# Linear attention into a Swish layer on one core: one order for all pieces, denominators from a gram product, loads by token quarter

## The chip, the cores and the metric

The kernel runs on 1 core of one Trainium2 chip. The metric is device time in microseconds (us), the median of the runs. TensorE (PE) multiplies matrices; VectorE (DVE), ScalarE (ACT) and GpSimd (POOL) do the elementwise work; SyncE (SP) issues most of the loads and stores. Each engine works through its own instructions strictly in the order in which the program gives them, and waits on semaphores for the others.

## The reference

Inputs are q, k, v of shape (4 batches, 4 heads, 1088 tokens, 32), two 8x32 matrices S1 and S2, and the layer's w_in (128x2048), w_out (2048x128) and beta (2048).

```python
def phi(x):                                  # 64 features of a token
    a = einsum('rd,bhsd->bhsr', S1, x)
    b = einsum('rd,bhsd->bhsr', S2, x)
    return einsum('bhsi,bhsj->bhsij', a, b).reshape(..., 64)
q_p, k_p = phi(q), phi(k)
kv = einsum('bhsf,bhsd->bhfd', k_p, v)
z = sum(k_p, axis=2)
x = einsum('bhsf,bhfd->bhsd', q_p, kv) / (einsum('bhsf,bhf->bhs', q_p, z) + 1e-6)
x = x.transpose(0, 2, 1, 3).reshape(4352, 128)
h = x @ w_in
out = (h / (1 + exp(-beta * h))) @ w_out
```

The sum over tokens in kv and z runs over a whole batch and head, so no token of a batch has its x before all of that batch's k and v are in.

## The kernel before

**The layer.** beta is folded into the weights: winp = w_in times beta, woutp = w_out divided by beta, both f16, so that g = silu(x winp) and out = g woutp. The 4352 tokens make nine chunks, eight of 512 and one of 256. Each chunk has eight waves, 72 in all. A wave is W (`w1`, L388: two 512-wide matmuls, in the first four waves four 256-wide ones, into one of two PSUM buffers `wave`), G (`silu`, L404: ACT reads that buffer and writes g in f16, six buffers) and V (`w2`, L419: the matmuls into `moeout`). O (`turn_out`, L433) turns a finished chunk on DVE and SP stores it. I call the nth of each W0, W1 and so on, from 0. W8 is the first wave of the second chunk and needs tokens 512 to 1023 in xT.

**The attention.** DVE turns k and q in blocks of 32x32 (`turn_k`, L442; `turn_q`, L448), PE projects them with S1 and S2 (`kps`, `qps`, L478), DVE turns the projections token by token (`turn_ab`, L499), and `outer` (L507, on POOL or DVE) multiplies a by b into the 64 features. `kv` (L555) multiplies features of k with v over the tokens. In batches 2 and 3 z is the sum of k's features on POOL (`sum_z`, L741 to L745), and the features of q are turned back (`turn_qo`, L518) for two matmul groups, `den_g` (L832) and `num_g` (L846); DVE inverts the denominators (`invert`, `spread_rc`, L767 to L782) and multiplies (`divide_g`, L857). In batch 1 and the second part of batch 0, called chunks B, C and D, the features of q never become token-major: `spread` (L531) makes a and b feature by feature in PSUM, ACT or DVE copies one (`asb`, L542), DVE multiplies (`mult`, L548), and `den0` (L756) and `num0` (L791) follow; batch 1's z comes from a gram product of its k projections on PE (`gram`, L692; `gram_z`, L714). The first 512 tokens of batch 0 (two halves of 256) take squares instead: products a*b as differences of two squares (`spread_sq`, L665; `square`, L674; `sq_mm`, L680); their z comes from k^T k on PE (`kk`, L576, 136 instructions) through `kk_s2`, `z_terms`, `z_sum` (L595 to L614).

**The order of the work** is written out by hand: `ORDER` (L1117) is a list of names, and every name emits its instructions, DMAs included, at that place. A leading point marks the pieces of the start. It begins with warm matmuls on unused data (`keep_warm`, L204: six ahead of the list, two in it).

**Loads.** At the top of the program SP issues nearly all of them at once: batch 0's k in two parts with beta and half of q between, v of batch 0 by head (four DMAs of 144 KB, `load_v`, L143), half of w_in and w_out, the rest of q, and so on through batch 2. A wait of one load on SP holds all that stand behind it.

Of the kernel before, what the change touches and what calls it, by code (L numbers as in the profile page):

```python
# [9 lines left out]
F32 = mybir.dt.float32  # L10
F16 = mybir.dt.float16
ACTF = mybir.ActivationFunctionType
MUL = mybir.AluOpType.mult

P = 128
# [3 lines left out]
def kernel(  # L19
# [12 lines left out]
    nc = tc.nc  # L32
# [10 lines left out]

    NJK = 9
    TH = T // 2
# [4 lines left out]

    NA = 16
    q_chk = {"B": (0, 16, 9), "C": (1, 0, 9), "D": (1, 18, 8)}
    QW = 32 * 9
    NJ0 = 5
    HA = 16 * NA

    QB = [0, 9, 16, 25]
    JW = 32 * NJK
    JR = [(0, 2), (2, 4), (4, 6), (6, 9)]
    WARM0 = 6  # L60
# [4 lines left out]
    ld = ctx.enter_context(tc.tile_pool(name="ld", bufs=3))  # L65
# [9 lines left out]

# [20 lines left out]
    beta4 = sb([P, DFF // 4], F32, "beta4")  # L96
# [3 lines left out]
    s12 = sb([2 * R, H, D], F32, "s12")  # L100
# [3 lines left out]
    def load_s(n, s_, eng):  # L104
        eng.dma_start(
            out=s12[R * n : R * n + R],
            in_=bass.AP(tensor=s_.tensor, offset=s_.offset, ap=[[D, R], [0, H], [1, D]]),
        )

    load_s(0, S1, nc.scalar)  # L110
    load_s(1, S2, nc.scalar)
    k_t, q_t, v_t = {}, {}, {}

    def load_rows(src, dst, b, tag, parts=((0, T),)):
        if b not in dst:
            dst[b] = ld.tile([P, TPAD, D], F32, tag=tag, name=tag)
        for t0, t1 in parts:
            nc.sync.dma_start(
                out=dst[b][:, t0:t1, :],
                in_=bass.AP(  # L120
                    tensor=src.tensor,
                    offset=src[b, 0].offset + t0 * D,
                    ap=[[T * D, P], [1, (t1 - t0) * D]],
                ),
            )

    def load_k0(j0, j1):
        if 0 not in k_t:
            k_t[0] = ld.tile([P, TPAD, D], F32, tag="k", name="k")
        nc.sync.dma_start(  # L130
            out=cut(k_t[0], [[NJK * D, 4], [1, (j1 - j0) * D]], j0 * D),
            in_=bass.AP(
                tensor=k.tensor,
                offset=k[0, 0].offset + j0 * D,
                ap=[[T * D, P], [NJK * D, 4], [1, (j1 - j0) * D]],
            ),
        )

    def load_v(b):
        t = v_t[b] = ld.tile([P, H, NJK, D], F32, tag="v", name="v")  # L140
        if b < B - 1:
            for h in range(H):
                nc.sync.dma_start(  # L143
                    out=t[:, h],
                    in_=bass.AP(
                        tensor=v.tensor, offset=v[b, h].offset, ap=[[NJK * D, 4], [T * D, 32], [1, NJK * D]]
                    ),
                )
            return
        nc.gpsimd.memset(t[96:, :, NJK - 2 :, :], 0.0)  # L150
        for g in range(4):
# [10 lines left out]
    def load_win(c0, c1):  # L162
        nc.sync.dma_start(out=w_in_sb[:, c0:c1], in_=moe_w_in[:, c0:c1])

    beta_bc = sb([P, DFF // 2], F32, "beta_bc")

    def load_beta():
        nc.sync.dma_start(
            out=bass.AP(
                tensor=beta4.tensor,  # L170
                offset=beta4.offset,
                ap=[[32 * beta4.ap[0][0], 4], [1, DFF // 4]],
            ),
            in_=moe_beta.rearrange("(r c) -> r c", r=4),
        )

    def load_wout(j0, j1):
        nc.sync.dma_start(
            out=w_out_sb[:, j0:j1, :],
            in_=moe_w_out[j0 * P : j1 * P, :].rearrange("(j p) m -> p j m", p=P),  # L180
        )

    load_k0(0, NJ0)
    load_beta()
    load_rows(q, q_t, 0, "q", ((0, NA),))
    load_k0(NJ0, NJK)
    load_v(0)
    load_win(0, DFF // 2)
    load_wout(0, NJ // 2)
    load_rows(q, q_t, 0, "q", ((NA, T),))  # L190
    load_rows(k, k_t, 1, "k")
    load_win(DFF // 2, DFF)
    load_wout(NJ // 2, NJ)
    load_rows(q, q_t, 1, "q")
    load_v(1)
    load_rows(k, k_t, 2, "k")
    load_rows(q, q_t, 2, "q")
    load_v(2)


    def keep_warm(n):
        t = bank(1, "warm")
        for _ in range(n):
            nc.tensor.matmul(out=t, lhsT=idle, rhs=cut(idle, [[0, 4], [1, P]]), start=True, stop=True)  # L204
# [3 lines left out]
    nc.gpsimd.dma_start(out=beta_jp, in_=moe_beta.rearrange("(j p) -> j p", p=P))  # L208
    ones = sb([P, P], F32, "ones")
    nc.vector.memset(ones, 1.0)  # L210
    silu0 = sb([P, 1], F32, "silu0")
    nc.scalar.activation(out=silu0, in_=ones[:, :1], func=ACTF.Silu)

    hm = sb([P, 2], F32, "hm")
# [3 lines left out]
    gm = sb([P, 4], F32, "gm")  # L218
    nc.vector.memset(gm, 0.0)
    for c in range(4):  # L220
        nc.vector.memset(gm[32 * c : 32 * c + 32, c : c + 1], 1.0)
    pm = sb([P, 2], F32, "pm")
    nc.vector.memset(pm[:, 0:1], 0.25)
    nc.vector.memset(pm[:, 1:2], -0.25)
    sg = sb([P, 2], F32, "sg")
    nc.vector.memset(sg, 0.0)
    nc.vector.memset(sg[:64, 0:1], 4.0)
    nc.vector.memset(sg[64:, 1:2], -4.0)
    sgs = sb([P, 1], F32, "sgs")
    nc.vector.memset(sgs[:64], 4.0)  # L230
    nc.vector.memset(sgs[64:], -4.0)
    eps = sb([P, 4 * NJK], F32, "eps")
    nc.vector.memset(eps, 1e-6)
    e3 = sb([P, 3], F32, "e3")
    nc.vector.memset(e3, 0.0)
    nc.vector.memset(e3[:, 1:2], 1.0)
# [4 lines left out]
    zb = [sb([P, H, 32], F32, f"zb{n}") for n in range(2)]  # L241
    mk = sb([P, H, R], F32, "mk")
    zbg = [sb([P, H, 2, 32], F32, f"zbg{n}") for n in range(2)]

    def clear():
        for n in range(2):
            nc.gpsimd.memset(kT2[n][:, T:, :], 0.0)
        for n in range(2):
            nc.gpsimd.memset(zb[n], 0.0)
            nc.gpsimd.memset(zbg[n], 0.0)  # L250
        nc.gpsimd.tensor_tensor(
            out=mk,
            in0=cut(ident, [[2 * R, H], [1, R]]),
            in1=cut(ident, [[2 * R, H], [1, R]], 64),
            op=mybir.AluOpType.add,
        )

    keep_warm(WARM0)
# [5 lines left out]
    spm = sb([P, 2, R, R], F32, "spm")  # L264
    s1pm = sb([P, 2 * R], F32, "s1pm")
    sab = [sb([P, R, R], F32, f"s{n}") for n in range(2)]

    def spread_s():
        t = bank(2, "srep")
        nc.tensor.matmul(  # L270
            out=t[:, : 2 * R],
            lhsT=s12.rearrange("p h d -> p (h d)"),
            rhs=ident[: 2 * R, : 2 * R],
            is_transpose=True,
            start=True,
            stop=True,
        )
        PS["srep"] = t
# [4 lines left out]
    def s_block():  # L283
        nc.gpsimd.tensor_tensor(
# [3 lines left out]
    def s_sums():  # L288
        ADD, SUB = mybir.AluOpType.add, mybir.AluOpType.subtract
        for n, op in enumerate((ADD, SUB)):  # L290
            nc.gpsimd.tensor_tensor(
                out=spm[:, n], in0=cut(st, [[1, R], [0, R]]), in1=cut(st, [[0, R], [1, R]], R), op=op
            )

    def s_pairs():
        nc.gpsimd.tensor_tensor(
# [5 lines left out]
        nc.gpsimd.tensor_tensor(  # L302
            out=s1pm.rearrange("p (m c) -> p m c", m=2),
            in0=cut(st, [[0, 2], [1, R]]),
            in1=cut(pm, [[1, 2], [0, R]]),
# [3 lines left out]
    def spread_factors():  # L309
        for n in range(2):  # L310
            nc.gpsimd.tensor_copy(out=sab[n], in_=cut(st, ([[1, R], [0, R]], [[0, R], [1, R]])[n], n * R))

    def beta_mm(n, dst):
        row = slice(32 * n, 32 * n + 1)
        nc.tensor.matmul(out=dst, lhsT=ones[row, :], rhs=beta4[row, :], start=True, stop=True)
# [5 lines left out]
    def prep_win(c0, c1, scale=None, eng=None):  # L321
        (eng or nc.gpsimd).tensor_tensor(  # L322
            out=winp[:, c0:c1],
            in0=beta_bc[:, c0:c1] if scale is None else scale,
            in1=w_in_sb[:, c0:c1],
            op=MUL,
        )

    def prep_rbeta():
        bt = bank(0, "bt")  # L330
# [3 lines left out]
        PS["bt"] = bt  # L334
# [14 lines left out]

    xT = sb([P, NTOK], F16, "xT")  # L350

# [11 lines left out]
    ALT = 6  # L363

# [17 lines left out]
    def w1():  # L382
        wave = ci, t0, o, w, j0, jn, head, tail = waves[moe["w"]]
        per = jn // 2
        wv = psm.tile([P, 2, TCH], F32, tag="wave", name="wave")
# [12 lines left out]
    def silu():  # L398
# [4 lines left out]
        gw = per * w  # L403
        nc.scalar.activation(out=g[:, :, :gw], in_=wv[:, :, :gw], func=ACTF.Silu)  # L404
        moe["todo"].append((wave, [g[:, jj // per, (jj % per) * w : (jj % per + 1) * w] for jj in range(jn)]))
        moe["g"] += 1

    def w2():
        wave, g = moe["todo"].pop(0)
        ci, t0, o, w, j0, jn, head, tail = wave  # L410
        if head:
            if ci >= ALT and (ci - ALT) % 2:
                t = pools()["ps1"].tile([P, TCH], F32, tag="one", name="moeout1")
# [26 lines left out]

    def turn_k(b, t0=0, t1=T):
# [11 lines left out]
    PS, KP, QO, QT, QP, ND, KAB, QAB, ASB, KVZ, KVD, RB = ({} for _ in range(12))  # L453

    def wave2(name):
        return psm.tile([P, 2, 512], F32, tag="wave", name=name)

    late = {}

    def pools():  # L460
        if not late:
            start.close()
            for n in ("ps2", "ps1", "pso"):
# [700 lines left out]
```

## Time and profile before

| | us |
|---|---|
| median of 3 runs | 115.93 (115.67 to 115.98) |
| span of the profiled execution | 116.5 |
| PE busy, 1316 matmul instructions | 105.3 |
| DVE busy | 57.5 |
| ACT busy, of it 72 silus | 79.9, 66.6 |
| POOL busy | 42.9 |
| HBM read and written | 8.94 MB, 2.23 MB |

The profiled execution has no time of its own beside its span, the time from its first to its last instruction; that stands 0.5 us above the median of the runs. A line of the timeline gives start, duration, engine, line, operation, tiles (out<-in) and shape, and in brackets the idle time before it and who ended it. An f32 matmul counts as two instructions. A busy PE is not PE at its peak, since its records overlap. The mean granted clock of the execution is 0.971 of full speed.

### The profile page before, as it was taken

To read this page: it belongs to the slowest core of one execution; us is meant where nothing else is said; L and a number is where in the kernel's file an instruction comes from. 1 tells how busy PE (TensorE), PEld (TensorE's weight loads), DVE (VectorE), ACT (ScalarE), POOL (GpSimd) and SP (SyncE) were. 2 spreads that over 40 slices of the span, in tenths; PEclk is the share of its full clock that TensorE was granted. 3 is DMA by queue.
4 is the path that set the end of the run, shared out by engine and by line. 5 is a ranking of instruction groups with operands and counts; after the bars stand their busy time and mean duration, and the time that the engine had idled before them with its cause. 6 is when DMAs were issued, how large, how long until landed. Compare 5 with 4: busy or idle time off the path is not lost.

```text
span 116.5 us, 3190 instructions
## 1 busy us (share of the span) xinstructions
PE 105.3 (90%) x1316; PEld 48.8 (42%) x1316; DVE 57.5 (49%) x122; ACT 79.9 (69%) x107; POOL 42.9 (37%) x61
## 2 busy tenths in 40 slices
PE   6898179898899999999999999999999989999960
PEld 2276055234434443344343354454344434444540
DVE  4384003588499754887899483529087020020210
ACT  4037002486868977555787975999986999999950
POOL 4036069230960099999399974000000000000000
PEclk9999955799999999999999999999999999999999
DMA  2859998279229975202300014005001303213242
GB/s 62 232 153 253 286 355 286 107 200 239 103 101 214 213 202 151 37 0 43 53 8 0 0 17 75 4 0 90 6 0 32 58 0 52 44 17 62 35 69 45
DMA packets 25046, 11.37 MB, mean 98 GB/s; under 512 B 18612, under 2 KB 23748, under 8 KB 25032
## 3 DMA queue, kind: packets, MB, share of 16 engines
q1 hardware_dynamic: 24376, 11.09, 38.8%
q8 instruction: 10, 0.16, 0.6%
q10 hardware_dynamic: 624, 0.07, 0.4%
q14 instruction: 4, 0.03, 0.1%
q0 software_dynamic: 32, 0.01, 0.1%
HBM read 8.94 MB, written 2.23 MB: 96 GB/s over the span
## 4 chain that ended last, share of the span: by engine, by line
PE 75%; DMA 10%; DVE 6%; SPq 4%; issue 2%; DVEq 0%
PE wave L388 25%; PE moeout L419 24%; DMA v<-in_v_dram 8%; PE kvz L555 5%; PE nps L846 3%; PE dps L832 2%; PE aps L531 2%; PE bps L531 2%; DVE o_sb L433 2%; DMA out_dram<-o_sb 2%; PE nps L791 2%; PE dps L756 2%; PE ndps L750 1%; SPq L143 1%; SPq L372 1%
## 5 line engine op out<-in xcount | busy, mean ns | idle before, releaser
L404 ACT ACTIVATE g<-wave 128x1024 f16<-128x1024 f32 (+1 forms) x72 | 66.6, 979 | 14.7 <-PE wave L388 13.2
L388 PE MATMUL wave<-xT,winp 128*128 128x512 f16 (+1 forms) x152 | 41.0, 357 | 0.9 <-DVE xT L918 0.5
L419 PE MATMUL moeout<-g,woutp 128*128 128x512 f16 (+1 forms) x152 | 39.6, 357 | 0.9 <-ACT woutp L1062 0.5
L388 PEld LDWEIGHTS <-winp 128*128 128x128 f16 x152 | 13.6, 97 | 19.5 <-issue 9.4
L507 POOL TENSOR_TENSOR kp<-kab 128x512 f32<-128x512 f32 (+2 forms) x15 | 15.6, 1068 | 16.3 <-DVE kab L499 13.6
L419 PEld LDWEIGHTS <-woutp 128*128 128x128 f16 x152 | 14.1, 98 | 16.4 <-issue 3.1
L433 DVE STREAM_TRANSPOSE o_sb<-moeout 128x512 f32<-128x512 f32 (+1 forms) x9 | 6.2, 687 | 26.2 <-PE moeout L419 22.8
L555 PE MATMUL kvz<-kp,v 128*32 128x64 f32 x288 | 7.3, 241 | 3.8 <-DMA v<-in_v_dram 3.0
L555 PEld LDWEIGHTS kvz<-kp,v 128*32 128x32 f32 x288 | 5.4, 121 | 7.1 <-DMA v<-in_v_dram 3.4
L507 POOL TENSOR_TENSOR qo<-qab 128x512 f32<-128x512 f32 (+1 forms) x7 | 7.8, 1131 | 0.7 <-DVE qab L499 0.7
L782 DVE STREAM_TRANSPOSE rb<-rc 128x576 f32<-128x576 f32 (+2 forms) x9 | 6.0, 678 | 0.1
L518 DVE STREAM_TRANSPOSE qt<-qo 128x512 f32<-128x512 f32 (+1 forms) x8 | 5.7, 746 | 0.0
L448 DVE STREAM_TRANSPOSE qT<-q 128x1088 f32<-128x1088 f32 (+2 forms) x5 | 5.3, 1060 | 0.6 <-DMA q<-in_q_dram 0.6
L548 DVE TENSOR_TENSOR qp<-bps,asb 128x576 f32<-128x576 f32 (+1 forms) x6 | 4.1, 730 | 2.4 <-PE bps L531 2.4
L767 DVE STREAM_TRANSPOSE dT<-dps 128x288 f32<-128x288 f32 (+1 forms) x6 | 2.7, 458 | 4.5 <-PE dps L832 2.9
L741 POOL TENSOR_TENSOR z<-kp 128x1024 f32<-128x1024 f32 x2 | 4.7, 2370 | 0.2
L204 PE MATMUL warm<-idle 128*128 128x512 f16 x8 | 3.7, 589 | 1.1 <-DVE idle L102 1.1
L322 POOL TENSOR_TENSOR winp<-beta_bc,w_in_sb 128x256 f16<-128x256 f32 x4 | 2.8, 728 | 5.0 <-DMA w_in_sb<-in_moe_w_in_dram 5.0
L857 DVE TENSOR_TENSOR xT<-nps,rb 128x576 f16<-128x576 f32 x4 | 3.0, 757 | 3.0 <-PE nps L846 2.9
L767 DVE STREAM_TRANSPOSE dT<-den 128x256 f32<-128x256 f32 x1 | 0.4, 449 | 8.0 <-PE den L680 8.0
L624 ACT COPY zq<-zq_ps 128x128 f32<-128x128 f32 x1 | 0.3, 265 | 5.6 <-PE zq_ps L614 5.6
L647 ACT COPY kab<-kab 128x320 f32<-128x320 f32 (+1 forms) x2 | 0.8, 398 | 4.7 <-PE kab L638 4.7
(119 smaller groups left out, 103.7 us busy)
## 6 DMA issues: line engine op xcount, KB each, us to landing
v<-in_v_dram SPq DMA_DIRECT2D x15, 144.0 KB, 10.2
k<-in_k_dram SPq DMA_DIRECT2D x3, 544.0 KB, 9.7
q<-in_q_dram SPq DMA_DIRECT2D x3, 544.0 KB
out_dram<-o_sb SPq DMA_DIRECT2D x20, 64.0 KB, 2.5
w_in_sb<-in_moe_w_in_dram SPq DMA_DIRECT2D x2, 512.0 KB
w_out_sb<-in_moe_w_out_dram SPq DMA_DIRECT2D x2, 512.0 KB
k<-in_k_dram SPq DMA_DIRECT2D x1, 320.0 KB
q<-in_q_dram SPq DMA_DIRECT2D x1, 288.0 KB
```

Source lines behind the costliest of these rows:

```text
L388: nc.tensor.matmul(out=wv[:, jj // per, c : c + w], lhsT=winp[:, (j0 + jj) * P : (j0 + jj + 1) * P], rhs=xT[:, t0 + o : t0 + o + w], start ...
L404: nc.scalar.activation(out=g[:, :, :gw], in_=wv[:, :, :gw], func=ACTF.Silu)
L419: nc.tensor.matmul(out=moe["acc"][-1][:, o : o + w], lhsT=woutp[:, j0 + jj, :], rhs=g[jj], start=head and jj == 0, stop=tail and jj == jn - 1,
L433: nc.vector.transpose(out=o_sb[:, :nt, :].rearrange("p t d -> p (t d)"), in_=moe["acc"].pop(0)[:, :tw])
L448: nc.vector.transpose(out=qT2[b % 2][:, t0:t1].rearrange("p t s -> p (t s)"), in_=q_t[b][:, t0:t1].rearrange("p t d -> p (t d)"),)
L507: (eng or nc.vector).tensor_tensor(out=cut(dst[b][:, j0:j1], [[F, n], [R, R], [1, R]]), in0=cut(a0 if first is None else first, [[2 * R, n ...
L518: nc.vector.transpose(out=QT[b][:, j0:j1].rearrange("p j h c s -> p (j h c s)"), in_=QO[b][:, j0:j1].rearrange("p j h f -> p (j h f)"),)
L531: nc.tensor.matmul(out=dst[64 * c : 64 * c + 64, m, : 32 * tn], lhsT=(sa if which == "a" else sb_)[rows, :], rhs=qT2[b % 2][rows, t0 + c * ...
L548: nc.vector.tensor_tensor(out=QP[n][:, :, pr], in0=bps[:, :, :w], in1=ASB[n, pr][:, :, :w], op=MUL)
L555: nc.tensor.matmul(out=KVZ[b][32 * h : 32 * h + 32, :F], lhsT=v_t[b][:, h, j, :], rhs=KP[b][:, j, h, :], start=(j == 0), stop=(j == NJK - ...
L741: eng.tensor_tensor(out=z4, in0=kp[:, 0:4], in1=kp[:, 4:8], op=ADD)
L782: nc.vector.transpose(out=rb, in_=cut(rc, [[1, n * tn], [0, 32]], i * tn))
```

## The change

The whole attention part is rewritten; the layer's W, G, V and O stay as they are. What it does:

- **Loads.** k of batch 0 is one DMA. v of every batch is loaded by g, a quarter of the tokens (four DMAs of 32 partitions with all four heads), as only batch 3's was before. Only k, half of q, v of batch 0 and half of w_in are issued at the top; each other load stands in `ORDER`, behind a memset of one column of its tile on POOL (so SP waits for that memset). S2 and beta go by POOL's queue, S1 by ACT's. The pool `ld` has 4 buffers of each tile.
- **beta** is spread over the partitions once, early: four f32 products of 512 columns, K=1, into both wave buffers (`beta_mm`), two 1024-wide copies on ACT. Before, two rows were spread at the start and two later.
- **No warm matmuls at the start**; six stand behind W1.
- **den from a gram product.** For each batch `gram` multiplies k's token-major projections: sum over tokens of b a^T. From it `w_mm` makes, per head, a third projection w of q, so that den = sum over the 8 rows of a*w. q is projected with S1, S2 and w at once (`qps`, 16 products with 32 rows and 32 columns), turned token-major (`turn_qab`), and DVE forms the 8 terms, sums them along the row and inverts (`den_terms`, `den_sum`); a is scaled by the result (`scale_a`), so that no division follows num. `sum_z`, `den_g`, `den0` and `invert` of these tokens are gone.
- **Token-major features of q** in the second part of batch 0 (four overlapping groups of 5) and in batches 1 to 3: outer, `turn_qo`, `num` (64 instructions per batch), and `put_x`, a copy from PSUM to xT, which `ORDER` gives to ACT in all eight places. `spread`, `asb`, `mult` are gone.
- **First 512 tokens:** still squares, but z from the gram of the token-major k (`gram_terms`, `z_mm`); `kk` and what hangs on it are gone. kab is 9 products instead of 18.

```diff
 def load_v(b):
     t = v_t[b] = ld.tile([P, H, NJK, D], F32, tag="v", name="v")
-    if b < B - 1:
-        for h in range(H):
-            nc.sync.dma_start(out=t[:, h], in_=bass.AP(tensor=v.tensor,
-                offset=v[b, h].offset, ap=[[NJK * D, 4], [T * D, 32], [1, NJK * D]]))
-        return
     nc.gpsimd.memset(t[96:, :, NJK - 2 :, :], 0.0)
+    if b:
+        nc.gpsimd.memset(t[:, 0, 0, :1], 0.0)
     for g in range(4):
...
+def beta_mm():
+    t = PS["bb"] = [wave2("bb") for _ in range(2)]
+    for r in range(4):
+        nc.tensor.matmul(out=t[r // 2][:, r % 2], lhsT=ones[32 * r : 32 * r + 1, :],
+            rhs=beta4[32 * r : 32 * r + 1, :], start=True, stop=True, tile_position=(32 * r, 0))
...
+def w_mm(b):
+    t = PS["wz"] = bank(2, "wz") if b == 0 else one("wz")
+    for h in range(H):
+        nc.tensor.matmul(out=t[32 * h : 32 * h + 32, :R], lhsT=lw[:, h, :], rhs=gs[:, h, :],
+            start=True, stop=True)
...
+def qps(b):
+    t = PS["qps"] = [wave2("qps"), two("qps")]
+    n = 32 * QN[b]
+    for h in range(H):
+        rows = slice(32 * h, 32 * h + 32)
+        for g in range(4):
+            nc.tensor.matmul(out=t[h // 2][32 * g : 32 * g + 32, h % 2, :n], lhsT=qw[b][rows, :],
+                rhs=qT2[b % 2][rows, QB[b][g] : QB[b][g] + QN[b], :], start=True, stop=True)
...
+def den_terms(b, eng):
+    eng.tensor_tensor(out=pac[b % 2][:, :n, :R], in0=cut(a0, [[32, n], [1, R]]),
+        in1=cut(a0, [[32, n], [1, R]], 2 * R), op=MUL)
+def den_sum(b):
+    nc.vector.tensor_reduce(out=RC[b][:, :n], in_=pac[b % 2][:, :n, :], axis=..., op=ADD)
+    nc.vector.reciprocal(out=RC[b][:, :n], in_=RC[b][:, :n])
+def scale_a(b, eng):
+    eng.tensor_tensor(out=a0, in0=a0, in1=cut(RC[b], [[1, n], [0, R]]), op=MUL)
...
+def num(b):
+    t = PS["nps"] = [two("nps"), wave2("nps")]
...
+def put_x(b, i, eng):
+    eng(out=cut(xT[:, b * S + 32 * q0 :], [[32 * (q1 - q0), 2], [1, w]]), in_=PS["nps"][i][:, :, :w])
...
+    lk1 S0 Sc mk tk02 Sbg Spg tk01 lm cl bb by0c tk00 j2 tqA j1 y1v sq0 j0 lk y2v ok08v y0c Ssg s1 ok07v
+    sq3 gm0 ok00g by1c ok04v gt s0 li1 q1 ok05v ok01g gcc ok03g zm zc ok02g kv002 kv024 dA1 ok06v kv046
+    kv068 wi0g iA1 kv089 q0 dA0 kqc nq nc iA0 wz0 wc0v nA0 xA0 nA1 xA1 tk1 wi1g rb lqB W lq1 wi2g wi3g W
+    h lo0 G sq1 wi6g h h kd0c wi4v h rv wi5v h h G W G kp1 W W G lo1 tqB kt1 tq1 gm1 G lv1 oK11g gcv qp0
+    wz1 wc1c wi7g W qa00 qa01 G wo0g wo1g dt0v ds0 wo3c nd0 sa0v wo5c qp1 qa10 oq01v wo2g t01 ny0c W V V
+    qa11 oq00g t00 W dt1v oK13v V V lk2 lq2 wo4c wo6g V V G ds1 G oK12g V nm0 oK10g x00c sa1v oq13g x01c
+    tk2 kv109 wo7c lv2 oq11g W kd1c W V O G G oq10g kp2 kt2 W t13 G V W t11 nd1 W G G oq12g V oK22g t10
...
```

In the new order a name ends with its engine: v is DVE, c is ACT, g is POOL. bb is the beta product, s0 and s1 the squares' products, gm the gram, zm the product for z, kv the kv product, dA and nA den and num of the first 512 tokens, xA their xT, lk, lq, lv, li, lo the loads of k, q, v, w_in and w_out, tk and tq turns, kt and qa turns of projections, oK and oq outer products, t turns of q's features, nm num, x copies to xT, h a warm matmul.

## Prediction

> **What bounds the kernel now.** I read the page's busy slices and its chain shares first, then the chain in order of time, the busy time by stage, the DMA issues and the timeline.
>
> ```profile
> span 116.5 us, 3190 instructions
> ...
> PE   6898179898899999999999999999999989999960
> ...
> ACT  4037002486868977555787975999986999999950
> ...
> PEclk9999955799999999999999999999999999999999
> ...
> PE 75%; DMA 10%; DVE 6%; SPq 4%; issue 2%; DVEq 0%
> ```
>
> TensorE (PE) is full in nearly every slice (2.9 us each) from the seventh on; in the fifth it has a hole, with the clock at half behind it. The chain in order of time says what made the hole:
>
> ```profile
> 4.66 9.75 DMA v<-in_v_dram
> 14.41 0.04 issue
> 14.45 0.31 PE kvz L555 x5
> ...
> 21.89 0.43 DVE xT L918
> 22.33 0.14 issue
> 22.46 0.60 PE wave L388 x4
> ```
>
> The last piece of v lands at 14.4, the kv product ends at 18.4, and den, nd and num follow one after the other until the first tokens xT (21.9) let the first wave of the second layer (W0) start at 22.46.
>
> ```profile
> 12.50:15.00 2.50, 0.47 (x7) 0.15 (x7) 0.00 (x0) 0.00 (x0) 0.00 (x0) 0.99 1.05 309
> 15.00:17.50 2.50, 1.93 (x39) 1.53 (x42) 0.00 (x0) 0.09 (x1) 1.81 (x3) 0.50 1.09 352
> 17.50:20.00 2.50, 2.50 (x45) 1.47 (x42) 0.63 (x3) 0.78 (x4) 2.32 (x10) 0.50 0.91 309
> 20.00:22.50 2.50, 2.02 (x18) 0.50 (x15) 1.25 (x5) 1.08 (x2) 0.40 (x1) 0.65 0.33 115
> ...
> 40.00:75.00 35.00, 35.00 (x529) 14.98 (x527) 25.09 (x44) 25.58 (x32) 27.02 (x23) 1.00 0.24 54
> 75.00:112.70 37.70, 36.98 (x250) 17.36 (x247) 10.43 (x17) 34.31 (x40) 0.00 (x0) 1.00 0.21 36
> ```
>
> Columns are length, then busy time of PE, PEld, DVE, ACT and POOL, granted clock, DMA share and GB/s. PE does 0.47 us in the 2.5 us before 15.0, then runs at clock 0.50 until past 20. From 40 to 75 it is busy all 35.0 us while ACT has 25.6; from 75 on ACT has 34.3 of 37.7. So there are four stretches: the head to W0 (22.5 us, v and the clock); W0 to the ninth wave W8, which needs the second half of the first batch (22.46 to 37.33, a chain through DVE); W8 to the last moeout at 112.7, where PE is the bound (75.4 us); and the tail of 3.8 (turn, store, landing).
>
> ```profile
> 37.33 0.59 PE L388 MATMUL wave<-xT,winp 128*128 128x512 f16 x2
> ...
> 112.75 0.45 DVE L433 STREAM_TRANSPOSE o_sb<-moeout 128x256 f32<-128x256 f32 x1 [3.36 <-DMA out_dram<-o_sb]
> ```
>
> **The head.** Batch 0's v was loaded by head; now it is loaded by quarter of the tokens (g), right behind k and the first q.
>
> ```profile
> v<-in_v_dram SPq DMA_DIRECT2D x15, 144.0 KB, 10.2
> ...
> k<-in_k_dram SPq DMA_DIRECT2D x1, 256.0 KB, 4.3
> ```
>
> A 144 KB piece of v took 10.2 us from issue, a 256 KB piece of k 4.3. Ahead of and with v now stand 544+256+576 = 1376 KB; at the 241 GB/s of the stretch 2.5 to 5 that ends at 8.2 us, at the best rate shown (352) at 6.4. I take 8.2. At 10.2 us after the last issue (about 4) it would be 14. [...]
>
> With v out of the way the rest has to be walked, in order on each engine:
> - S comes half by POOL's queue (beta_jp there: 3.0 us to landing), so at 3.7; the spread of S ends at 4.1. beta4 is second there, 1.4+3.0 = 4.4.
> - All four beta rows are now spread at once, ahead of kab: 8 instructions where L315 has 4 in 1.13 us, 2.3 us at full clock, 4.5 at half; four 256-wide products in four row groups took 0.71 (L665), which gives 1.4 for 512. I take 3.4, between the clocks: 4.5 to 7.9. Everything on PE is queued behind it.
> - kab: 18 instructions (36 took 1.49), to 8.9. sq for half 1: 0.7 to 1.24 (L665 at both clocks), to 9.75. Gram of k: 18 instructions, 0.70 (L692), to 10.5 behind the kab copies.
> - DVE then has two copies, the L mask and three outer products at 0.41 (128x256, L507) ahead of the gram terms, which end at 11.2; z product 0.56 (L714's 16 instructions) 11.9; its copy, first half of kv, den of half 1 (0.64) 13.25; rest of kv 14.0 (72 instructions, 1.3 in all); den of half 0 14.65. The old 136 kk instructions (2.4 us) and its chain u, zt, zq are gone.
> - copy of kv 0.26, turn 0.41, copy 0.27, num 0.64, with 0.15 to 0.2 at each change of engine: num ends at 16.35, xT at 16.9, **W0 at 17.1**: 5.4 earlier.
>
> The eight warm matmuls at the start (clock 1.00 by 5 us) are gone; now they come only behind W1. In before PE worked from 15.6 and the mean of 0.65 in 20 to 22.5 puts the clock back at about 21.7, 6 us later; from 4.5 on that gives 10.6, and I have used full clock from about 10. With the clock at half all the way the matmuls from kv on cost 2.8 us more and W0 comes at 19.8; at full from the start, about 16. [...]
>
> **W0 to W8.** xT's second half, tokens 512 to 1087 of batch 0, now goes by token-major features. On DVE in order from 16.5: two xT (0.42 each), k turn 1.29, two winp 0.42, rbeta 0.25, q turn 0.72, kab turns 0.92, q turn 1.29, gram copy 0.16, two qab turns (320 wide) 1.0, den terms 0.33, sum and reciprocal 0.6, scaling 0.33, qab turn 0.76 (576 wide, L782), outer 0.69, qo turn 0.67, qab turn 0.76, qo turn 0.97: 12.4, less about 1 that neighbours overlap, plus short waits: 11.7, ending 28.25. Then num (half of L846's 1.53, rounded up to 0.9), two ACT copies to xT (0.42 each for 320 wide), changes 0.4: **W8 at 30.5**, 13.4 behind W0 where it was 14.9. Only ACT and PE's first eight waves lie beside it. A sum along the row is not in the trace: from 0.29 (128 wide) to 0.76 (576 wide); I take 0.35. POOL has its outer of 1.5 done at 26.4, under this. The loads now wait for a one-column memset on POOL; behind a waiting load on SP stand the later loads and the stores. POOL reaches them at 13 to 16 us, so q, w_out and v of batch 1 land by 16 to 23, before use. If POOL were late there, W8 would be late by as much.
>
> **W8 to the end.** Work on PE beside the second layer, from the chain of before: kvz 0.58, kps and qps 2.6, gram and zc 1.26, aps and bps 2.58, dps 0.62+0.57+2.22, nps 0.65+0.59+3.07, kvz of two batches 2.77, ndps 1.29: 18.8. After: batch 1 has kv 1.28, nd 0.29, num 1.53; batches 2 and 3 each kps 0.65, gram 0.70, w 0.2, qps 0.77, kv 1.28, nd 0.29, num 1.53, so 5.4: in all 13.9. So 4.9 goes: den is summed on DVE instead. qps is 16 tiles of 32x32, half of num's 64 instructions: 0.77; it lies between 0.65 (L478) and 1.53 each, at most 1.5 more for two. w is between 0.11 (L728) and 0.31 (L595). 75.4 − 4.9 = 70.5. ACT has there 56 silus at 0.94 (five in 4.69 at 97.2) and 8 at 0.58, 57 us, plus six copies to xT at 0.64 (L542), w_out 0.78 and small ones: 63. DVE has some 35. Both stay below PE, but num and qps each take one of the two wave buffers, so I add 1.5 of PE waiting (0 to 5).
>
> **The sum.** 17.1 + 13.4 + 70.5 + 1.5 + 3.8 = 106.3 against the execution's span of 116.48; the runs' median 115.93 is 0.5 below that span, so 105.8.
>
> **The rivals.**
> - *The head stays slow*: clock at half to W0 and beta in 4.5 us, or v late after all (the load change does not do what it says): kv behind 14 gives W0 at 19 to 20, 108 to 110. For it: no warm-up, and a long product at the front of PE's queue. Against: that product keeps PE busy. 0.18.
> - *The order packs better*: W0 at 16, a DVE chain with more overlap (-1.5), no waits (-1.5): 101.5 to 104. For it: DVE spaces 0.76 us operations 0.68 apart at 35.8. 0.12.
> - *A new wait behind W8*: the xT copies now sit in ACT's queue between silus and hold a wave buffer and a PSUM pair; with 0.5 to 1 us for each of 8 copies, 110 to 113.5. For it: ACT goes from 73% toward 90% in the middle. Against: before, asb and xT on DVE held the same buffers. 0.08.
> - *Half clock until W8* (the other side): PE between W0 and W8 has 11.7 us of work; at clock 0.50 that is 23 in a stretch of 13.4, 10 more, and 2.7 in the head: 118 to 119, slower. [...] For it: 15 to 17.5 was 77% busy and did not bring the clock back. Against: the head of before from 5 to 12 held 1.0 with such work, and 17.5 to 21.7 brought it back; at half clock the gaps close. 0.06. [...]
>
> **Numbers.** The forecast (104 to 108.5) has 0.56. About 0.3% is what a measurement of this kernel can tell from no change. Slower by more: the slow clock's 0.06 and 0.02 for a new wait that runs on past 116, 0.08; within: another 0.02 of it; faster: 0.90. The range 101.5 to 111 leaves out the slow clock, most of the new wait and what packs better still.
>
> **What would show it.** W0 near 17 and W8 near 30.5 in the timeline; no DMA v in the chain; the beta product 2 to 4.5 us long at about 4.5; the clock at 1.0 from about 10; PE over 95% busy from W8 on; 3.8 after the last moeout. W0 past 20, a clock of 0.5 behind W0, or PE gaps before qps and num would prove me wrong.

## The result and the profile after

The changed kernel takes 116.63 us (median of 20 runs, 115.95 to 117.4), the kernel before 116.42 beside it; the ratio is 1.0064, with a 95% interval of 1.0034 to 1.0093: no gain, and by this interval a loss of 0.3 to 0.9%. Forecast were 105.8 us and a range of 101.5 to 111.0. The profiled execution took 116.47 us with a span of 114.6. From the page of its profile:

```profile
span 114.6 us, 3043 instructions
...
PE   0059999969999699999999999999999989999940
...
ACT  3103160416989198966899978978897999999920
...
PEclk9999999999999999999999999999999999999999
...
PE 58%; ACT 16%; DVE 13%; DMA 6%; issue 3%; ACTq 0%; POOLq 0%
```

TensorE now does nothing in the first two slices, and v is no longer in the chain. The row of the granted clock shows full speed throughout. That is misleading: the trace's clock record has its first entry at 22.2 us, a change to full speed, and the row shows full speed for the time ahead of it as well. The durations below are those of half clock. The chain of waits, in order of time (start, length, what), shows the head as it was:

```profile
1.27 5.35 DMA s<-in_S_dram
...
6.71 0.34 PE srep L236 x8
...
8.16 1.73 PE bb L295 x5
9.89 4.03 PE kab L469 x18
13.92 2.02 PE sq L687 x8
15.94 1.20 PE gram L537 x18
17.14 2.02 PE sq L687 x8
19.16 1.00 PE zqps L721 x16
20.15 1.01 PE kvz L523 x32
21.17 0.90 PE den L701 x8
...
26.14 0.87 PE wave L391 x7
```

From 7.4 to 22 TensorE is on the path without a break, and each step is long: 32 kvz instructions take 1.01 us where 72 take 1.43 later on (at 54.5), and 8 square instructions 2.02 where an experiment below has 1.14. By stage, in us (before: the profile that the prediction used, and a second one, taken as an experiment):

| | before | before, again | forecast | after |
|---|---|---|---|---|
| span | 116.5 | 113.9 | 106.3 | 114.6 |
| head, to W0 | 22.5 | 19.5 | 17.1 | 26.1 |
| W0 to the last moeout | 90.2 | 90.7 | 85.4 | 84.0 |
| tail | 3.8 | 3.8 | 3.8 | 4.5 |

W8 is at 41.2 in the profile after, so of the 84.0 us 15.1 lie ahead of it (13.4 forecast) and 68.9 behind it (72.0 forecast). What lies between W0 and the last moeout became 6.2 to 6.7 us shorter, a little better than forecast; the head became 3.6 to 6.6 us longer and took it back.

### The profile page after: what moved, and what is told of

It is laid out like the page before. It is cut to its first block, busy times and chain, and to the rows that moved or that the text cites. A ratio compares the mean times of both kernels' runs of the same rounds, so it can differ in the third digit from the quotient of the medians.

```text
span 114.6 us, 3043 instructions
## 1 busy us (share of the span) xinstructions
PE 100.0 (87%) x1244; PEld 52.8 (46%) x1244; DVE 57.7 (50%) x122; ACT 79.9 (70%) x103; POOL 39.1 (34%) x77
## 4 chain that ended last, share of the span: by engine, by line
PE 58%; ACT 16%; DVE 13%; DMA 6%; issue 3%; ACTq 0%; POOLq 0%
PE wave L391 18%; ACT g L408 16%; PE moeout L423 13%; DMA s<-in_S_dram 5%; PE nps L659 4%; PE kab L469 4%; PE sq L687 4%; PE kvz L523 3%; PE gram L537 3%; DVE qab L604 2%; PE kps L491 2%; PE qps L592 2%; DMA out_dram<-o_sb 2%; PE bb L295 2%; DVE qt L647 1%
## 5 line engine op out<-in xcount | busy, mean ns | idle before, releaser
L391 PEld LDWEIGHTS <-winp 128*128 128x128 f16 x152 | 13.8, 97 | 18.8 <-issue 8.6
L423 PEld LDWEIGHTS <-woutp 128*128 128x128 f16 x152 | 14.6, 97 | 13.6
L437 DVE STREAM_TRANSPOSE o_sb<-moeout 128x512 f32<-128x512 f32 (+1 forms) x9 | 6.2, 685 | 26.4 <-PE moeout L423 24.7
L511 POOL TENSOR_TENSOR kp<-kab 128x512 f32<-128x512 f32 (+2 forms) x12 | 11.4, 967 | 16.1 <-PE wave L391 9.2
L637 POOL TENSOR_TENSOR qo<-qab 128x512 f32<-128x512 f32 (+1 forms) x10 | 12.6, 1280 | 4.5 <-DVE qab L630 4.4
L647 DVE STREAM_TRANSPOSE qt<-qo 128x512 f32<-128x512 f32 (+1 forms) x14 | 10.5, 768 | 1.4 <-POOL qo L637 1.3
L671 ACT CAST xT<-nps 128x576 f16<-128x576 f32 (+1 forms) x8 | 4.7, 586 | 4.9 <-PE nps L659 4.8
L659 PE MATMUL nps<-qt,nd 32*32 32x288 f32 (+1 forms) x256 | 6.0, 385 | 1.0 <-DVE qt L647 1.0
L305 ACT COPY beta_bc<-bb 128x1024 f32<-128x1024 f32 x2 | 2.0, 1014 | 6.7 <-PE bb L295 6.7
L604 DVE STREAM_TRANSPOSE qab<-qps 128x576 f32<-128x576 f32 (+1 forms) x8 | 5.4, 693 | 1.6 <-PE qps L592 1.5
L511 DVE TENSOR_TENSOR kp<-kab 128x256 f32<-128x256 f32 (+2 forms) x9 | 5.5, 647 | 0.0
L637 DVE TENSOR_TENSOR qo<-qab 128x512 f32<-128x512 f32 (+1 forms) x4 | 4.3, 1083 | 0.8 <-POOL qab L630 0.8
L659 PEld LDWEIGHTS nps<-qt,nd 32*32 32x32 f32 x256 | 3.2, 103 | 3.3 <-issue 1.5
```

Source lines behind the costliest of these rows:

```text
L391: nc.tensor.matmul(out=wv[:, jj // per, c : c + w], lhsT=winp[:, (j0 + jj) * P : (j0 + jj + 1) * P], rhs=xT[:, t0 + o : t0 + o + w], start ...
L423: nc.tensor.matmul(out=moe["acc"][-1][:, o : o + w], lhsT=woutp[:, j0 + jj, :], rhs=g[jj], start=head and jj == 0, stop=tail and jj == jn - 1,
L437: nc.vector.transpose(out=o_sb[:, :nt, :].rearrange("p t d -> p (t d)"), in_=moe["acc"].pop(0)[:, :tw])
L511: eng.tensor_tensor(out=cut(KP[b][:, j0:j1], [[F, n], [R, R], [1, R]]), in0=cut(a0, [[2 * R, n], [1, R], [0, R]]), in1=cut(a0, [[2 * R, n] ...
L604: nc.vector.transpose(out=cut(QAB[b], [[32, 2], [32 * H, nq], [1, 32]], 64 * pr), in_=PS["qps"][pr][:, :, : 32 * nq],)
L637: eng.tensor_tensor(out=cut(QO[b][:, j0:j1], [[F, n], [R, R], [1, R]]), in0=cut(a0, [[32, n], [1, R], [0, R]]), in1=cut(a0, [[32, n], [0, ...
```

## The experiments

**The kernel before, once more.** 

> The kernel before, unchanged, profiled a second time. The profile that the prediction was summed on had a span of 116.5 us and was set 0.5 us above the median of three times (115.93). Each profiled run of the changed kernel lasts 1.9 us longer than its span, so a typical execution of the kernel before should have a span of about 114.5. Theory A: the profile used was one of the longer executions of this kernel, and this one has a span of 114 to 115.5; the prediction's step from span to median was then 2 us short. Theory B: the span comes out at 116 to 117 again with a time near 116, and the step stands.

Span 113.9, time 115.88; the spans of its 8 runs go from 113.7 to 116.3, each 1.9 to 2.0 us under its time, and the two longest have the mean granted clock of the first profile, 0.971. Theory A holds (113.9 lies just under its 114). The clock opened at 12.1 us here; in the first profile it opened at 4.7, fell at 14.9 and came back at 21.8.

**Idle products ahead.** In the order of the pieces:
```
-lk1 S0 Sc mk ...
+lk1 HA S0 Sc mk ...      # HA: 16 products of idle, 128x512 f16, into bank 1
```


> The changed kernel with 16 idle 128x512 f16 products ahead of the spread of S, so that TensorE works from 1.1 us until S lands at 6.6. Nothing else is changed. Clock theory: the head is long because TensorE runs at half clock until 22.2 us; with full clock from about 5, the products between 7.4 and 22.2 take little more than half, the first wave starts at 20 to 21.5 in place of 26.1, and the time is 111 to 112.5. Rival: the landings of S and the chain of VectorE and GpSimd (block of S, mask, kab copies, outer products, inverse) hold the head; then the first wave stays at 24 or later and the time is above 114.5. If the clock falls back in a gap behind the spread of S, as it did in the kernel before at 14.9, the trace's matmul durations will show where.

W0 at 24.3, 113.98 us, ratio 0.982 (0.978 to 0.987). W0 is 1.8 us earlier, less than half of what the clock theory expected (4.6 to 6.1). In stretches of about 3.4 us (columns: stretch and length, PE busy, granted clock, DMA share, GB/s):

```profile
4.00:7.30 3.30, 2.30 (x18) 1.00 1.08 264
7.30:10.70 3.40, 3.02 (x25) 1.00 0.80 283
10.70:14.10 3.40, 3.40 (x19) 0.50 0.00 1
14.10:17.50 3.40, 3.40 (x34) 0.50 0.52 159
17.50:20.90 3.40, 3.40 (x94) 0.50 0.85 230
```

The clock opened at 3.9, fell at 10.7 and stayed at half for 10.2 us in which TensorE was busy all the time. So it is not enough that TensorE has work; in the second stretch it was busy for 3.02 of 3.40 us, and the clock fell at its end.

**S2 on ScalarE's queue.** The load of S2 is moved from `nc.gpsimd` to `nc.scalar`, behind S1. 

> The changed kernel with the second half of S loaded by ScalarE's queue, behind the first half, as in the kernel before, and no longer by GpSimd's. Queue theory: S is whole at about 4 us in place of 6.6, the spread of S starts there, the first wave starts about 2.5 us earlier (23.5) and the time is about 114. Clock theory as a rival for the size: TensorE is still at half clock, it starts earlier and so its clock opens earlier too, and the gain can be 2.5 to 4 us; if k's landing holds the first kab products, it is under 2 us.

The spread of S starts at 5.2 in place of 6.7 to 7.2, W0 is at 24.6, the time 115.96 (1.000; 0.996 to 1.003). 4.0 for S was too early: behind S1 on one queue it lands at 4.4 to 5.2. W0 is 1.5 us earlier and the time 0.7 less than in the changed kernel, well under the queue theory's 2.5; the clock opened at 20.9.

**Both.** S2 moved, `HA` with 6 products, and 3 more behind the spread of S. 

> Both edits: the second half of S on ScalarE's queue, 6 idle products ahead of the spread of S and 3 behind it. If the two causes are all that was wrong with the predicted head, the first wave starts at 17.5 to 18.5 and the time is about 108.5. If the full-width kab products (18 in 4.0 us at half clock) are a third cause, they still take 2 us at full clock in place of the predicted 1.0 and the first wave comes at 18.5 to 20, time 109.5 to 110.5. If VectorE and GpSimd hold the head, the first wave is at 22 or later and the time above 113.

W0 at 25.1, 114.60 us (0.987; 0.982 to 0.991): the numbers of the third case, but not its reason, for TensorE was busy from 6.4 to 22.6. In the profiled execution six products (2.7 us) did not open the clock; it opened at 21.7, and kab took 4.1 us as in the changed kernel. Two of the four runs (114.67 and 114.06) have a mean clock of 0.939: there the clock must have opened early and then been at half for some 13.7 us (0.061 of 112.5 us, twice), and their time was hardly less. Something in the head had to keep the clock from opening.

**Narrow kab products.**
```
-    out=t[:, 64*(j-j0) : ...], lhsT=kT0[:, j]                      # 18 instructions
+for c in range(2):
+    out=t[64*c : 64*c+64, 64*(j-j0) : ...], lhsT=kT0[:, j, 2*c : 2*c+2]   # 36
```


> The changed kernel with kab made of 36 products of 64 columns, two side by side, as in the kernel before, in place of 18 products of 128 columns. Nothing else. Width theory: at half clock 36 took about 2.45 us in the second profile of the kernel before (1.33 + 1.12), and 18 wide ones 4.0 here, so the first wave comes 1.5 us earlier (24.5) and the time is about 115.1. If the width also decides whether the clock opens (narrow products side by side count as busy, wide ones that wait for their weights do not), the clock opens a window earlier as well and the time is 113 to 114. Rival: k's last landing or VectorE's transposes hold these products, and the gain is under 0.5 us.

112.62 us, ratio 0.961 (0.951 to 0.971). From the timeline (start, busy, operation):

```profile
10.23 2.19 PE L470 MATMUL kab<-sbd,kT 128*64 128x64 f32 x36
12.35 2.02 PE L688 MATMUL sq<-qT,spm 64*128 64x256 f32 x8
14.30 0.77 PE L538 MATMUL gram<-kab 128*64 128x32 f32 x18
15.00 1.14 PE L688 MATMUL sq<-qT,spm 64*128 64x256 f32 x8
```

kab is 1.9 us shorter at the same half clock, and the clock opened at 14.2: the second four squares take 1.14 where the first took 2.02, the gram 0.77 for 1.27. With wide products it opened at 20.9 to 22.2 in three executions in which it had not opened earlier. Width theory and its second clause hold in this execution, and the time is below the 113 to 114 that they gave; the four runs spread from 110.97 to 113.57, and only one was profiled.

**Idle products and narrow kab together.** 

> 16 idle products ahead of the spread of S (as in the run that opened the clock at 3.9 and lost it at 10.7) together with the 36 narrow kab products. If narrow products keep the clock open, it stays at full speed past 10.7, kab takes 1.5 us, and everything up to the first wave runs at full clock: first wave at 19.5 to 21, time 110.5 to 112. If the clock still falls at about 10.7 because the products of beta, of the squares and of the gram are also not busy enough, the first wave comes at 23 to 23.5 and the time is 113 to 113.5.

109.22 us, 0.942 (0.935 to 0.950). Three of the four runs took 109.06 to 109.23, with a mean clock of 0.995 to 0.999: better than expected. In the profiled one (111.41) the clock opened at 3.7, fell at 10.5 and came back at 17.4, with W0 at 21.9: the mechanism of the second outcome does occur, at a smaller price than expected.

**Idle products throughout.** Moved S2, 8 idle products ahead of the spread of S and 2 behind it, narrow kab, and 9 products ahead of kab, squares, gram and z. 

> All causes found so far are treated at once: the second half of S on ScalarE's queue, 8 idle products ahead of the spread of S and 2 behind it, narrow kab products, and idle products (128x512 f16, written to the bank that the real product then overwrites) ahead of each kab group (1), each square product (2), the gram (1) and z (1). They cost 9 times 0.22 = 2.0 us of TensorE at full clock. If dense products keep the clock open through the head, the first wave comes at 18 to 20 and the time is 109 to 111. If the clock falls back all the same, the idle products cost 0.43 each, the first wave comes at 25 or later and the time is at that of the changed kernel.

111.45 us (0.963; 0.956 to 0.969), W0 at 21.9: between the two expectations. The clock opened at 5.1, fell at 8.5 in the weak stretch of the spread of S and beta, and came back at 11.9. That is 2.7 us above the same kernel without the 9 products, which comes next.

**The same without the 9 products.** 

> The run with idle products ahead and narrow kab products, and the second half of S on ScalarE's queue as well (8 idle products ahead of the spread of S, 2 behind it; none further on). Queue theory: S is whole at 4.9 in place of 6.9, beta's product starts at 6.5 (it then waits for beta) in place of 8.0, so everything up to the first wave comes 1.5 us earlier: time 107.5 to 108, against 109.2. Rival: the clock falls back in the weak stretch of the spread of S and of beta (as it did at 8.5 in the run with idle products throughout), and the 1.5 us are lost again: time 109 to 111.5.

108.77 us (0.941; 0.935 to 0.946). The clock fell at 7.5, behind a wait of 0.84 us for beta, and came back at 10.9: the rival happened, and 0.45 of the 1.5 us was left.

**Squares in another order.** `for h in (0, 2, 1, 3)` in spread_sq. 

> The run with all three edits of the head (8 and 2 idle products, narrow kab, S on ScalarE's queue), and the four products of each square in the order of heads 0, 2, 1, 3, so that products of the lower and the upper 64 rows follow each other and can run side by side. At half clock 8 instructions took 2.0 us, at full clock 1.14; side by side they take about half. Theory: 0.5 us is saved twice at full clock (1.0 twice at half clock), and the denser products keep the clock open: 1 us below the same kernel without this order, 106.5 to 107. Rival: the second square waits for its load, ScalarE's square or the gram anyway, and the time is the same within 0.4.

108.42 us, 0.937 (0.930 to 0.943); the profiled execution 108.00. The theory is wrong: the squares take 1.14 and 1.13 as before, nothing ran side by side. In this execution the clock opened at 5.8 and did not fall:

```profile
5.01 0.30 PE L241 MATMUL srep<-ident,s 16*32 16x16 f32 x8 [0.36 <-DMA s<-in_S_dram]
...
7.55 1.27 PE L475 MATMUL kab<-sbd,kT 128*64 128x64 f32 x36
8.77 1.14 PE L693 MATMUL sq<-qT,spm 64*128 64x256 f32 x8
9.83 0.77 PE L543 MATMUL gram<-kab 128*64 128x32 f32 x18
...
18.30 1.05 PE L396 MATMUL wave<-xT,winp 128*128 128x256 f16 x8
```

W0 is at 18.3 and the span is 106.2. This kernel and the one of the preceding experiment are the fastest measured; they beat both kernels of the comparison, and 0.9365 and 0.9405 do not tell them apart.

**v by rows alone.** In the kernel before, `if b < B - 1` in load_v becomes `if b < 0`, so that all batches load by g. 

> The kernel before with one part of the change alone: v of batches 0 to 2 is loaded by rows (four transfers by g) and no longer by head. Two profiles of the kernel before differ: in one TensorE's clock opened at 4.7 us, the k part was done at 10.8, it waited for v for 3.0 us and the clock fell back at 14.9; in the other it opened only at 12.1 and v was waited for 0.3 us. Theory: rows land by 9, so neither wait remains; the first wave comes at 18 to 19.5, and the median falls by 1 to 3 us (113 to 115) with a smaller spread. Rival: k, beta and q land later since v now takes all 16 engines from them, and the time stays within 0.5 us of the kernel before.

117.59 us, ratio 1.011 (1.001 to 1.021): if anything slower, by about 1%, against both theories. v landed 4.5 to 4.8 us behind its issue, by 9, and yet (chain of waits):

```profile
10.62 0.38 PE kvz L555 x10
11.00 3.77 issue
14.77 1.07 PE kvz L555 x30
```

"issue" says that no semaphore ended the wait. In this profile and both of the kernel before the pause lies behind the same 449th recorded instruction of TensorE, and in the record of DMA packets the first 16 KB block of the instruction queue q8 runs from 12.2 to 13.4 here (12.7 to 14.1 and 12.5 to 13.8 in the others). TensorE goes on 1.41 to 1.45 us after the end of that block in all three (14.77, 15.57 and 15.19). The author's reading is that it had run out of instructions, and that in the kernel before the wait for v hid this; no run tested that, nor what sets the block's time.

**v by head in the changed kernel.** The old branch of load_v put into the run with idle products and narrow kab. 

> The run with idle products ahead and narrow kab products, with v of batches 0 to 2 loaded by head again, as in the kernel before; the later loads stay late. Layout theory (by head a load runs on few DMA engines): v of batch 0 lands after 9 us or more, at about 12 to 13, just ahead of its products (14 to 15 at full clock), and v of the later batches lands after 8 to 10 us; time the same to 1 us more. Traffic theory (v was late in the kernel before because all other loads were issued at the same time): v lands within 6 us by head too, and the time is the same within 0.4.

109.50 us (0.950; 0.937 to 0.962). The time fits both theories; the landings do not. The four pieces of v were issued at 1.7, 2.4, 3.0 and 3.6 us, and by the landing updates in the trace they were in at 7.0, 9.4, 11.5 and 13.4, just ahead of their products:

```profile
13.45 0.65 PE L538 MATMUL kvz<-kp,v 128*32 128x64 f32 x32
```

In the stretch from 4.0 to 7.3 the DMA engines are busy for half the share that they have in the run with v by rows (first line here, second line there; columns as above):

```profile
4.00:7.30 3.30, 2.91 (x23) 1.00 0.48 137
4.00:7.30 3.30, 2.22 (x18) 1.00 1.07 259
```

The layout theory holds, for the landings and for the share of the DMA engines. The last piece by head lands 9.8 us behind the start of its issue with late loads, and 9.8 to 9.9 among early loads in the two profiles of the kernel before; by rows a piece takes 4.5 to 4.8 among early loads and 5.3 to 5.6 with late ones. The trace also shows how they land: a piece by head is told of by one update within 1.1 us of its issue and four when its data is in; a piece by rows, in the preceding experiment, by sixteen. In the packet records of the two kernels of the comparison, 4.1 packets of batch 0's v are under way at a time by head (mean from 5.8 to 13.6 us) and 9.6 by rows (4.0 to 7.8). The pieces by head come in one after the other, 1.9 to 2.4 us apart. So later loads alone do not bring v in time; here it was in time by less than 0.1 us, because the kv products start at 13.45.

**Both outer products of q on VectorE.** `oq00g` becomes `oq00v`. 

> The run with idle products ahead and narrow kab products, and both outer products of q of batch 0 on VectorE, one after the other; GpSimd makes none of them. Contention theory: VectorE's 128x512 outer product took 1.51 us only because GpSimd's 128x768 ran at the same time; alone it takes 0.69 and the 768 one 0.95, 1.64 in all, so the first one's transpose starts 0.8 us earlier and the second's at most 0.3 later, for the same time (109.2, within 0.5). Rival: 1.51 is what VectorE takes for this operation with these operands; then the two take 1.5 and 2.2, the second transpose comes 2 us later, and the time rises by 0.5 to 2.

Timeline, VectorE and then GpSimd:

```profile
29.06 1.42 DVE L643 TENSOR_TENSOR qo<-qab 128x512 f32<-128x512 f32 x1
...
31.82 0.92 DVE L643 TENSOR_TENSOR qo<-qab 128x768 f32<-128x768 f32 x1
```
```profile
28.87 2.54 POOL L517 TENSOR_TENSOR kp<-kab 128x512 f32<-128x512 f32 x2
```

The larger product, with GpSimd idle, takes 0.92; the smaller one takes 1.42, for GpSimd had moved on to an outer product of k in that time, and one of those two is stretched too (2.54 for two; 2.09 in the changed kernel). The contention is shown. Its form looks like a wait and not like a lower rate: taking 1.07 us for one of GpSimd's two products (its time alone, at 24.7), the first ends at 29.94, and VectorE's ends 0.54 us behind that; in the changed kernel VectorE's ends at 36.52, 0.55 behind GpSimd's at 35.97. The larger product's rate would give 0.61 for 512 elements. No run was made to settle this.

The time, 111.54 (0.958; 0.939 to 0.976), is 2.3 above the run it was built on, more than either theory had. In the profiled execution the clock fell at 34.1 and came back at 37.5. Three of the four runs have a mean clock of 0.980 to 0.984 and took 111.5 to 111.6; the fourth, with 0.997, took 109.90. So most of the 2.3 us goes with the clock; the other 0.7 stays open.

## Why the prediction was wrong

**The step that failed is "I have used full clock from about 10".** It came at 22.2. The prediction weighed the lost warm-up and relied on the row from 5 to 12 us of the kernel before, which "held 1.0 with such work". That work was another: kab there is 64 columns wide, two products side by side; here kab is 128 wide. And the row was that of one execution: in the second profile of the kernel before, the same work ran at half clock until 12.1. The 6 us from the start of work to full clock were also those of that one execution (from 15.6 to 21.8). In the changed kernel TensorE worked 15 us without a gap, from 7.4 to 22.2, before the clock opened; and with 16 idle products ahead it fell in the middle of work, at 10.7.

**The head, term by term** (9.0 us over the forecast, by the chain above):
- S: the spread was put at 3.7, it starts at 6.7: 3.0 late. "Half by POOL's queue, 3.0 us to landing" was read from beta_jp, on the same queue at nearly the same time (issued at 1.44 there, at 1.27 here); this one took 5.35, and why is not shown. But removed alone it gives only 1.5 us earlier, and at full clock W0 is at 18.85 with it and at 18.30 without.
- beta: 3.8 us from the spread of S to the end, 2.8 measured: 1.0 better. The row groups do run side by side: at full clock 8 instructions take 1.14 (first experiment with idle products), where the kernel before has 1.13 for 4.
- kab: "18 instructions (36 took 1.49)", 1.0 us; 4.03 measured: 3.0 late. The price per instruction was carried over from narrow to wide products. At full clock the 36 narrow ones take 1.27.
- the first squares, gram, second squares and z: 6.2 us where 3.0 were counted: 3.2 late. At full clock the same stretch takes 3.9 (8.8 to 12.8, with the squares in another order), so 2.3 are the clock; the other 0.9 was mis-sized, and TensorE waits 0.43 of it for VectorE's gram terms.
- from z to W0: 0.8 late.

With full clock and narrow kab, W0 is at 18.3 to 18.85, within 1.2 to 1.75 of the forecast 17.1. So 7.2 of the 9.0 us are the clock and the width of kab together. They are no sum of two: idle products alone give 1.8, narrow products alone 3.9, both 7.2 where the clock held, and 4.1 in the profiled execution of the first run with both, where it fell at 10.5.

**v**: the time was right (8.2, at the latest 8.6 measured), and the choice of it over 14. By head the data of a piece comes with four landing updates and by rows with sixteen; the last piece by head takes 9.8 us among early and among late loads, a piece by rows at most 5.6. What the prediction had wrong is the worth of that wait: without it the kernel before runs into the pause at its 449th instruction.

**W0 to W8** was 1.7 us longer than forecast: VectorE's outer product took 1.51 in place of 0.69 (0.8; the row it was priced by has one input in PSUM, and took 0.69 although GpSimd was busy beside it); the other steps of VectorE add up as forecast, to 11.7 us, and the other 0.9 is overlap that did not come and waits (0.76 for the second num, 0.54 without a releaser). **W8 to the end** was 3.1 shorter; TensorE idles 0.8 us in it where 1.5 were added, and how the other 2.3 divide between work done earlier and cheaper products was not separated. **The tail** has 0.7 more.

**From span to time.** "0.5 below that span" compared one of the longest executions of the kernel before with the median of others. Each run's time is 1.9 us above its span. The forecast span of 106.3 would have been 108.2 us, and 108.00 is what the repaired head gives (span 106.2). That is partly luck: W0 is 1.2 later there than forecast, and what lies behind it 1.3 shorter.

Of the rivals, "the head stays slow" named the place but was sized for "half clock to W0" at products priced too low (108 to 110). "Half clock until W8" was wrong in place: the clock was back 4 us ahead of W0. "A new wait behind W8" did not come: that stretch beat its forecast.

## What to carry to other kernels

Before a warm-up is dropped, ask what the first microseconds of TensorE will consist of: here 128-wide f32 products and squares kept it busy in the profile from 9.8 us on, and yet the clock opened only at 22.2; the same product in two narrow halves side by side was shorter (2.19 us for 4.10, at half clock), and in that run the clock opened at 14.2. Read a cold start from the durations of equal instructions early and late, not from the clock row. When a wait is taken away, look for what it covered.

## What the runs showed of the hardware

The clock's changes lie whole multiples of 3.41 us apart in every trace (10.24 and 6.83 in both the kernel before and the run with 16 idle products; 3.41 in four others); such a step of 3.41 us is called a window below. When the clock changes differs from execution to execution; of the two profiles of the kernel before, 2.5 us apart in span, one opened it at 4.7 and lost it from 14.9 to 21.8, and the other opened it at 12.1 and did not lose it.

What decides a change is not settled. Counted back from each change in steps of 3.41 us, a window filled with wide kab products and squares did not open the clock in four traces, nor did one of squares and gram in the profiled run with idle products and narrow kab; one of narrow kab products and squares did in two, and the first window made mostly of z, kv and den products did in all four with wide kab. The spread of S with beta's one-row products lost the clock in three traces with narrow kab (at 10.5, 8.5 and 7.5) and kept it in three others. The weight loads do not tell the two kinds of kab apart: they fill 3.9 of the 4.1 us of the wide products and 2.0 of the 2.2 us of the narrow ones.

VectorE's outer product with both inputs in SBUF took longer beside GpSimd: 128x512 in 1.51 us (1.42 in the last experiment), against 0.92 for one and a half times that size with GpSimd idle, and 0.69 for that size in the kernel before, where one input came from PSUM and GpSimd was busy too. By elements, an estimate from the 0.92, the product took 2.3 to 2.5 times as long here. The cause was not shown.

In the kernel before with v by rows, TensorE paused for 3.77 us in the middle of the head with no semaphore to end the wait, until 1.4 us after the end of a 16 KB block of the instruction queue (12.2 to 13.4). That the block came late for it is the author's reading of these times.

A load of v whose outermost count is 4 (by head) landed with four updates when its data was in, and the last of its four pieces 9.8 us behind its issue; one whose outermost count is 32 (by rows) landed with sixteen updates, 4.5 to 5.6 us behind its issue.
